# Moving the conversion of w_out to tiles 48 to 70, and two steps of the weight conversion to ScalarE, in a fused attention and gated-convolution kernel

## The chip, the cores and the metric

The kernel runs on one core of a Trainium2 chip. The metric is device time in microseconds (us) of one execution, as the median over several runs. One execution was also profiled; PE is TensorE, DVE is VectorE, ACT is ScalarE, POOL is GpSimd, SP is the engine whose queue issues nearly all DMAs.

## What is computed

```
q_bits = (q @ proj) > 0;  k_bits = (k @ proj) > 0        # 6 bits: a bucket per row
mask   = bucket(q_bits) == bucket(k_bits)
attn   = softmax(where(mask, q @ k.T / sqrt(64), -1e9))  # per batch and head: 768 x 768
x      = attn @ v, heads side by side                    # (4, 768, 512)
gate   = sigmoid(causal depthwise conv of x, 5 taps, conv_w)
out    = ((x @ w_val) * gate) @ w_out
```

There are 4 batches of 8 heads with 768 rows of 64 numbers. `w_val` and `w_out` are 512 x 512 and come as 64-bit floats, as does `conv_w`; everything else is 32-bit.

## The kernel before

**Tiles.** A unit is one (batch, head); there are 32. Each has 6 tiles of 128 query rows, so the main loop runs over 192 tiles k. For each tile PE makes the scores (L266) into a PSUM buffer `s` (two of them), DVE takes the row maxima (L272) and two small numbers from them, `gs` (L278) and `nb` (L282), ACT does the exponential (L290), POOL divides by the row sums (L305), PE transposes the result (L314), ACT copies it out of PSUM (L323), and PE multiplies it with v (L337). The scores of tile k + 1 need the buffer of tile k - 1, so PE can be held by the exponential, that by `nb`, and that by whatever stands ahead of the maxima in DVE's queue. Each engine executes its queue in the order of the program.

**Side work.** The loop advances several generators by a step now and then: `preps` (next unit's operands: L170, L173 on POOL and DMAs on SP's queue), `convs` (the convolution, L366 on POOL and L368 on DVE, and the rounding of x, L357 and L358), `moes` (the two products with the weights, L399 and L424, the first one of a batch from tile 67 on), `ahead` (bits of later units) and `weights`.

**The weight conversion.** Two generators of `load_weights` each take half of the eight parts (four 128-row parts of `w_val`, then four of `w_out`). A part is 128x512 numbers of 64 bits. It goes through seven steps: a DMA on SP's queue (L137); ACT takes the absolute value of the high words (L91, tile `o`); DVE clamps and shifts it (L93, L94); DVE puts the bits of the high words together (L97, in place in `w`); DVE takes the exponent (L100) and multiplies the low words with it and with a constant (L101); DVE casts to the rounded matmul type (L109, out to `wv` or `wo`); POOL makes the remainder (L111, L113). A staging tile `w` has two buffers, so the DMA of a part waits until POOL has finished an earlier one. How many steps a tile takes is a table in the main loop, seven steps per six tiles, turn by turn from the two generators. `outp`, the first user of `wo`, finishes what is left.

Of the kernel before, what the change touches and what calls it, by code (L numbers as in the profile page):

```python
# [10 lines left out]
AF = mybir.ActivationFunctionType  # L11
ALU = mybir.AluOpType
# [4 lines left out]
U32 = mybir.dt.uint32  # L17
# [9 lines left out]
def kernel(  # L27
# [10 lines left out]
    nc = tc.nc  # L38
    B, H, _, S = qk.shape
# [4 lines left out]
    NP = H // 2  # L44
    KW = 5
    LAG = 3
    scale = 1.0 / float(D) ** 0.5
# [15 lines left out]
    op = ctx.enter_context(tc.tile_pool(name="op", bufs=2))  # L63
# [23 lines left out]
    def from_float64(w, t):  # L87

        lo, hi = w[:, :, 0], w[:, :, 1]
        a, d, ti = hi.bitcast(FP32), lo.bitcast(FP32), t.bitcast(I32)  # L90
        nc.scalar.activation(out=t, in_=a, func=AF.Abs)  # L91
        yield
        nc.vector.tensor_scalar(out=t, in0=t, scalar1=LEAST, scalar2=None, op0=ALU.max)  # L93
        nc.vector.tensor_scalar(out=ti, in0=ti, scalar1=3, scalar2=0x3fffffff,  # L94
                                op0=ALU.logical_shift_left, op1=ALU.bitwise_and)
        yield
        nc.vector.scalar_tensor_tensor(out=hi, in0=hi, scalar=-2 ** 30, in1=ti,  # L97
                                       op0=ALU.bitwise_and, op1=ALU.bitwise_or)
        yield
        nc.vector.tensor_scalar(out=ti, in0=hi, scalar1=-2 ** 23, scalar2=None, op0=ALU.bitwise_and)  # L100
        nc.vector.scalar_tensor_tensor(out=d, in0=lo.bitcast(U32), scalar=2.0 ** -52, in1=t,  # L101
                                       op0=ALU.mult, op1=ALU.mult)
        return a, d

    def split_weight(w, hi, lo):
        if w.dtype == I32:
            a, d = yield from from_float64(w, op.tile([P, 512], FP32, name="o"))
            yield
            nc.vector.tensor_copy(out=hi, in_=a)  # L109
            yield  # L110
            nc.gpsimd.tensor_tensor(out=a, in0=a, in1=hi.bitcast(FP32), op=ALU.subtract)  # L111
            yield
            nc.gpsimd.tensor_tensor(out=lo, in0=a, in1=d, op=ALU.add)  # L113
        else:
            nc.scalar.copy(out=hi, in_=w)
            yield
            nc.gpsimd.tensor_tensor(out=lo, in0=w, in1=hi.bitcast(FP32), op=ALU.subtract)
# [10 lines left out]
        else:  # L128
            nc.sync.dma_start(out=cw_sb, in_=conv_w)

    def load_weights(which):
        parts = [(src[:, c, :], hl[0][:, c, :], hl[1][:, c, :])
                 for src, hl in ((w_val, wv), (w_out, wo)) for c in range(NP)]
        for src, hi, lo in parts[which::2]:
            if src.dtype == mybir.dt.int64:
                w = wst.tile([P, 512, 2], I32, name="w64")
                nc.sync.dma_start(out=w, in_=src.bitcast(I32).rearrange("p (n t) -> p n t", t=2))  # L137
            else:
                w = wst.tile([P, 512], FP32, name="w32")
                nc.sync.dma_start(out=w, in_=src)  # L140
            yield
            yield from split_weight(w, hi, lo)

    def load_raw(i):
        if i < len(units):
# [230 lines left out]
    def acc_tile():  # L376
        pools = accs
        pool, name = pools[0]
        pools.append(pools.pop(0))
        if name == "s":  # L380
            return pool.tile([P, 2, 512], FP32, name="s")[:, 0, :]
        return pool.tile([P, 512], FP32, name=name)

    def moe(b, xs_, g):
# [5 lines left out]
                todo.pop(0)()  # L390

        def val(o, j):
            acc = acc_tile()
            m = 0
            for wi, xi in ((0, 0), (1, 0), (0, 1)):
                if m:
                    yield
                for c in range(NP):
                    nc.tensor.matmul(out=acc[:, 0:HS], lhsT=wv[wi][:, c, j * P:(j + 1) * P],  # L399
                                     rhs=xs_[(c, o)][xi], start=(m == 0), stop=(m == 11))  # L400
                    m += 1
                later()
            ht = hp.tile([P, HS], FP32, name="ht", bufs=2)
            nc.vector.tensor_tensor(out=ht, in0=acc[:, 0:HS], in1=g[j][:, o:o + HS], op=ALU.mult)  # L404

            def split():
                hh = hp.tile([P, HS], FP32R, name="hh")
                nc.vector.tensor_copy(out=hh, in_=ht)  # L408
                hl = hp.tile([P, HS], FP32R, name="hl")
                nc.gpsimd.tensor_tensor(out=hl, in0=ht, in1=hh.bitcast(FP32), op=ALU.subtract)  # L410
                hs[(o, j)] = (hh, hl)
            todo.append(split)
            yield
# [48 lines left out]
    def step(gens):  # L462

        while gens:
            try:
                return next(gens[0])
            except StopIteration:
                gens.pop(0)
# [7 lines left out]
    with tc.manual_schedule(engines=ENGINES):  # L476
# [1 line left out]
            load_raw(i)  # L478
        load_values(0)
        first_prep()  # L480
        weights = [[load_conv(), load_weights(0)], [load_weights(1)]]
        preps = [first_bits(), prep(1)]
        scores(0)
        next(preps[1])
# [5 lines left out]
        for k in range(N + LAG + 1):  # L490
# [21 lines left out]
                exponentials(k)  # L512
            if k >= 60 or k % 2:
                step(convs)
            for _ in range((1, 0, 2, 0, 2, 2)[k % 6]):
                step(weights[turn])
                turn = 1 - turn

# [79 lines left out]
```

## Time and profile before

| | |
|---|---|
| median of 3 runs | 622.08 us (621.6 to 622.21) |
| the profiled execution: its span, first to last instruction | 620.8 us |
| PE busy | 585.5 us, 94% of the span |
| DVE busy | 437.6 us, 70% |
| ACT busy | 421.4 us, 68% |
| POOL busy | 395.6 us, 64% |

The profile gives no time of the profiled execution other than its span. A busy share is a mean over stretches that differ: up to tile 66 there is attention alone, with the conversion of the weights beside it, and from tile 67 on the products with the weights fill PE. So the table says little of a change in one stretch.

### The profile page before, as it was taken

The numbers are of one execution on the slowest core, as the hardware profiler recorded it, in microseconds if no ns is written. First come the engines' busy times: TensorE is split into PE (matmuls) and PEld (weight loads), VectorE is DVE, ScalarE is ACT, GpSimd is POOL, SyncE is SP. The second block draws the span as 40 slices with busy tenths as digits, with TensorE's granted clock in tenths as the row PEclk, the third lists the DMA queues.
The fourth block names the chain that finished last, engine by engine and source line by source line (L and its number), as shares of the span: only waits on it lengthen the run. The fifth ranks groups of instructions, "written<-read, shape, count | busy, mean of one in ns | idle before, by whom it ended". The sixth has DMA issues, their size and how long they took to land.

```text
span 620.8 us, 10648 instructions
## 1 busy us (share of the span) xinstructions
PE 585.5 (94%) x3496; PEld 423.4 (68%) x3496; DVE 437.6 (70%) x1017; ACT 421.4 (68%) x881; POOL 395.6 (64%) x373
## 2 busy tenths in 40 slices
PE   5789898989999999999999999999999999999997
PEld 2655565555657777776767777777667877775895
DVE  5869798998975866668575867569665877665532
ACT  2777777778778666777787676777787766765400
POOL 3576868778766765578564777568764777544321
PEclk9799999999999999999999999999999999999999
DMA  6467666564532235243433234333422213200111
GB/s 227 123 197 199 200 167 208 157 175 118 133 83 68 70 79 142 72 108 82 122 82 107 61 80 126 84 115 82 108 70 78 67 42 91 69 18 1 51 52 51
DMA packets 29031, 64.64 MB, mean 104 GB/s; under 512 B 4937, under 2 KB 10057, under 8 KB 28977
## 3 DMA queue, kind: packets, MB, share of 16 engines
q1 hardware_dynamic: 28832, 63.93, 37.8%
q8 instruction: 28, 0.46, 0.3%
q14 instruction: 27, 0.21, 0.1%
q10 hardware_dynamic: 144, 0.03, 0.0%
HBM read 30.60 MB, written 7.86 MB: 62 GB/s over the span
## 4 chain that ended last, share of the span: by engine, by line
PE 66%; DVE 12%; ACT 12%; DMA 5%; issue 3%; POOL 2%; SPq 1%; ACTq 0%; POOLq 0%; DVEq 0%
PE av L337 17%; PE s L266 16%; PE tp L314 12%; PE m L424 8%; PE m L399 7%; ACT p L290 5%; DVE nm L272 4%; ACT pt L323 3%; ACT x L345 2%; DMA w<-in_w_val_dram 2%; DVE g L368 2%; PE tp L399 1%; PE tp L424 1%; PE s L424 1%; DMA bk<-bq 1%
## 5 line engine op out<-in xcount | busy, mean ns | idle before, releaser
L305 POOL TENSOR_SCALAR p<-p,ri 128x768 f32<-128x768 f32 x192 | 210.5, 1100 | 156.0 <-DVE nb L282 130.8
L272 DVE TENSOR_REDUCE nm<-s 128x1 f32<-128x768 f32 x192 | 182.5, 950 | 61.2 <-PE s L266 61.0
L290 ACT ACTIVATE p<-s,nb,gs 128x768 f32<-128x768 f32 x192 | 192.6, 1003 | 46.2 <-DVE nb L282 41.9
L323 ACT COPY pt<-tp 128x384 f32<-128x384 f32 x384 | 165.7, 485 | 75.3 <-PE tp L314 74.4
L314 PEld LDWEIGHTS tp<-ident,p 128*128 128x128 f32 x1152 | 130.3, 142 | 72.2 <-issue 43.6
L314 PE MATMUL tp<-ident,p 128*128 128x128 f32 x1152 | 164.4, 279 | 2.6 <-ACT pt L323 2.1
L337 PE MATMUL av<-pt,vt 128*64 128x384 f32 x768 | 144.9, 498 | 0.0
L266 PE MATMUL s<-ak,aq 76*128 76x384 f32 x384 | 118.1, 389 | 23.2 <-ACT p L290 19.7
L266 PE MATMUL s<-bk,bq 128*128 128x384 f32 x384 | 101.3, 345 | 0.4 <-DVE bq L252 0.4
L337 PEld LDWEIGHTS av<-pt,vt 128*64 128x64 f32 x768 | 47.0, 136 | 61.5 <-issue 61.4
L266 PEld LDWEIGHTS s<-ak,aq 76*128 76x128 f32 x384 | 59.2, 194 | 38.7 <-ACT p L290 34.6
L368 DVE SCALAR_TENSOR_TENSOR g<-x,cw_sb,g 128x768 f32<-128x768 f32 x64 | 79.4, 1241 | 2.2 <-POOL g L366 2.1
L266 PEld LDWEIGHTS s<-bk,bq 128*128 128x128 f32 x384 | 71.7, 194 | 0.8 <-issue 0.8
L173 POOL TENSOR_TENSOR bq<-r,aq 128x768 fp32r<-128x768 f32 x31 | 59.2, 1909 | 0.1
L410 POOL TENSOR_TENSOR hl<-ht,hh 128x384 fp32r<-128x384 f32 x32 | 32.3, 1009 | 39.5 <-DVE hh L408 39.5
L345 ACT COPY x<-av 64x384 f32<-64x384 f32 x64 | 30.4, 475 | 29.7 <-PE av L337 29.0
L282 DVE TENSOR_SCALAR nb<-nm,gs 128x1 f32<-128x1 f32 x192 | 40.4, 211 | 3.5
L399 PE MATMUL m<-xh,wv 128*128 128x384 f32 x200 | 42.7, 337 | 0.0
L358 POOL TENSOR_TENSOR xl<-x,xh 128x384 fp32r<-128x384 f32 x32 | 33.4, 1059 | 13.8 <-DVE xh L357 13.8
L290 ACT ACTIVATION_READ_ACCUMULATOR p<-s,nb,gs 128x1 f32 x192 | 39.0, 203 | 0.0
L404 DVE TENSOR_TENSOR ht<-m,g 128x384 f32<-128x384 f32 x25 | 13.9, 556 | 35.6 <-PE m L399 29.2
L424 PE MATMUL m<-wo,hh 128*128 128x512 f32 x144 | 38.1, 394 | 0.0
(86 smaller groups left out, 486.9 us busy)
## 6 DMA issues: line engine op xcount, KB each, us to landing
r<-in_qk_dram SPq DMA_DIRECT2D x32, 384.0 KB
vt<-in_v_dram SPq DMA_DIRECT2D x16, 384.0 KB
out_dram<-o SPq DMA_DIRECT2D x24, 256.0 KB
ak<-aq SPq DMA_DIRECT2D x31, 192.0 KB
bk<-aq SPq DMA_DIRECT2D x31, 192.0 KB
bk<-bq SPq DMA_DIRECT2D x31, 192.0 KB
bq<-aq SPq DMA_DIRECT2D x31, 192.0 KB
hh<-in_qk_dram SPq DMA_DIRECT2D x16, 192.0 KB
```

Of the source, the lines that this page charges most:

```text
L173: nc.gpsimd.tensor_tensor(out=bq, in0=r, in1=aq.bitcast(FP32), op=ALU.subtract)
L266: nc.tensor.matmul(out=s[:, hf, 0:HS], lhsT=lq[0:n, qs], rhs=rk[0:n, hf * HS:(hf + 1) * HS], start=n == M, stop=n == P)
L272: nc.vector.tensor_reduce(out=nm, in_=s[:, :, 0:HS], axis=AX.XY, op=ALU.max, negate=True)
L290: nc.scalar.activation(out=p, in_=s[:, :, 0:HS], func=AF.Exp, bias=nb, scale=gs.pop(k), accum_out=sm[:, k % 2, 0:1])
L305: nc.gpsimd.tensor_scalar(out=p, in0=p, scalar1=rcs.pop(k), scalar2=1.0, op0=ALU.mult, op1=ALU.mult)
L314: nc.tensor.transpose(out=tp[:, n * P:(n + 1) * P], in_=p[:, kb * P:(kb + 1) * P], identity=ident)
L323: nc.scalar.copy(out=pt[:, :, qo:qo + P], in_=tp[:, 0:HS].rearrange("p (a b) -> p a b", b=P))
L337: nc.tensor.matmul(out=av[s * D:(s + 1) * D, 0:HS], lhsT=vt[:, kb, hh * D:(hh + 1) * D], rhs=pt[kb // 3][:, kb % 3, :], start=(kb == 0), s ...
L345: nc.scalar.copy(out=x[hh * D:(hh + 1) * D, o:o + HS], in_=av[s * D:(s + 1) * D, 0:HS])
L368: nc.vector.scalar_tensor_tensor(out=g, in0=x[:, k:k + S], scalar=w, in1=g, op0=ALU.mult, op1=ALU.add)
L399: nc.tensor.matmul(out=acc[:, 0:HS], lhsT=wv[wi][:, c, j * P:(j + 1) * P], rhs=xs_[(c, o)][xi], start=(m == 0), stop=(m == 11))
L424: nc.tensor.matmul(out=acc, lhsT=hs[(o, j)][hi][:, tb * P:(tb + 1) * P], rhs=wo[wi][:, j, :], start=(m == 0), stop=(m == 11))
```

## The change

Three things are changed. The product on DVE of low words, exponent and constant (L101) becomes two instructions: ACT multiplies the low words by the constant, right behind the absolute value (new L92), and DVE multiplies that with the exponent (new L102, two inputs and no scalar). For `w_val` the cast to the rounded type is done by ACT and not by DVE. And each of the two generators becomes two, one for `w_val` and one for `w_out` behind it, with fewer steps per tile from tile 12 on, so that `w_val` ends at about tile 44 and `w_out` is converted at tiles 48 to 70; `val` finishes the `w_val` part first if it must.

```diff
         nc.scalar.activation(out=t, in_=a, func=AF.Abs)
+        nc.scalar.activation(out=d, in_=lo.bitcast(U32), func=AF.Copy, scale=2.0 ** -52)
         yield
...
-        nc.vector.scalar_tensor_tensor(out=d, in0=lo.bitcast(U32), scalar=2.0 ** -52, in1=t,
-                                       op0=ALU.mult, op1=ALU.mult)
+        nc.vector.tensor_tensor(out=d, in0=d, in1=t, op=ALU.mult)
         return a, d
...
-            nc.vector.tensor_copy(out=hi, in_=a)
+            cast(out=hi, in_=a)
...
         def val(o, j):
+            for gens in weights:
+                while len(gens) > 1:
+                    step(gens)
...
-        weights = [[load_conv(), load_weights(0)], [load_weights(1)]]
+        weights = [[load_weights(i, w_val, wv, nc.scalar.copy), load_weights(i, w_out, wo, nc.vector.tensor_copy)]
+                   for i in range(2)]
+        weights[0].insert(0, load_conv())
...
-            for _ in range((1, 0, 2, 0, 2, 2)[k % 6]):
+            for _ in range((1, 0, 2, 0, 2, 2)[k % 6] if k < 12 else (1, 0, 1, 0, 1, 1)[k % 6] if k < 48 else 1):
                 step(weights[turn])
                 turn = 1 - turn
```

What this does to the queues is seen in the order of the instructions. Line numbers behind L90 differ by one or so between the two kernels.

DVE at tiles 28 and 29, before: maxima are `nm`, the convolution is `g`, and the rows with `w` and `o` are the conversion.

```order
L93 TENSOR_SCALAR o<-o 128x512
L94 TENSOR_SCALAR o<-o 128x512
L109 CAST wv_120<-w_875 128x512
L229 TENSOR_SCALAR ht<-m,packed 128x384
L272 TENSOR_REDUCE nm<-s 128x1
L278 TENSOR_SCALAR gs<-nm 128x1
L282 TENSOR_SCALAR nb<-nm,gs 128x1
L368 SCALAR_TENSOR_TENSOR g<-x,cw_sb,g 128x768
L97 SCALAR_TENSOR_TENSOR w_994<-w_994,o 128x512
```

DVE at tiles 28 and 29, of the change.

```order
L228 TENSOR_SCALAR ht<-m,packed 128x384
L271 TENSOR_REDUCE nm<-s 128x1
L277 TENSOR_SCALAR gs<-nm 128x1
L281 TENSOR_SCALAR nb<-nm,gs 128x1
L367 SCALAR_TENSOR_TENSOR g<-x,cw_sb,g 128x768
```

Four instructions of the conversion no longer stand between these maxima and the next ones.

DVE at tiles 54 and 55, before.

```order
L272 TENSOR_REDUCE nm<-s 128x1
L296 TENSOR_SCALAR s_2166<-sm 128x2
L278 TENSOR_SCALAR gs<-nm 128x1
L300 RECIPROCAL ri<-s_2166 128x2
L282 TENSOR_SCALAR nb<-nm,gs 128x1
L272 TENSOR_REDUCE nm<-s 128x1
L278 TENSOR_SCALAR gs<-nm 128x1
L282 TENSOR_SCALAR nb<-nm,gs 128x1
L368 SCALAR_TENSOR_TENSOR g<-x,cw_sb,g 128x768
```

DVE at tiles 54 and 55, of the change.

```order
L281 TENSOR_SCALAR nb<-nm,gs 128x1
L101 TENSOR_SCALAR o<-w_1865 128x512
L102 TENSOR_TENSOR w_1865<-w_1865,o 128x512
L271 TENSOR_REDUCE nm<-s 128x1
L277 TENSOR_SCALAR gs<-nm 128x1
L281 TENSOR_SCALAR nb<-nm,gs 128x1
L367 SCALAR_TENSOR_TENSOR g<-x,cw_sb,g 128x768
L94 TENSOR_SCALAR o<-o 128x512
L95 TENSOR_SCALAR o<-o 128x512
```

Four instructions of `w_out` now stand here, two of them right behind a convolution step.

ACT at tiles 10 and 11, of the change; before, the row with L92 was not there and the other rows stood in the same order.

```order
L289 ACTIVATE p,sm<-s,nb,gs 128x768
L91 ACTIVATE o<-w_427 128x512
L92 ACTIVATE w_427<-w_427 128x512
L322 COPY pt<-tp 128x3x128 x2
L289 ACTIVATE p,sm<-s,nb,gs 128x768
```

The new multiplication stands ahead of the copies that free PE's transposes, and there are eight such places.

On DVE, before, L93 of a part stands at tiles 4, 11, 16, 23, 28, 35, 40 and 47 and its last L109 at tile 52; in the change the same step (L94 there) stands at tiles 4, 11, 17, 30, 38, 50, 55 and 64 and the last L109 at tile 70. ACT's L91 stands at tiles 2, 10, 14, 22, 26, 34, 38 and 46 before, and at 2, 10, 14, 28, 35, 48, 53 and 62 in the change; its four casts at 8, 18, 26 and 40. PE's order is the same in both, and its first use of `wo` stands behind the scores of tile 78. On SP's queue the load that the L91 of tile 10 reads stood behind the last of the four copies for the next unit (`bq<-aq`); in the change it stands ahead of the third (`bk<-bq`).

## Rows read from the trace of the kernel before

**Rows 1.** The page: span, busy time, and the chain that ended last, by engine.

```profile
span 620.8 us, 10648 instructions
PE 585.5 (94%) x3496; PEld 423.4 (68%) x3496; DVE 437.6 (70%) x1017; ACT 421.4 (68%) x881; POOL 395.6 (64%) x373
...
PE 66%; DVE 12%; ACT 12%; DMA 5%; issue 3%; POOL 2%; SPq 1%; ACTq 0%; POOLq 0%; DVEq 0%
```

**Rows 2.** Busy us by stretch: length, PE, PEld, DVE, ACT, POOL; clock, DMA share, GB/s.

```profile
42.80:76.50 33.70, 31.49 (x206) 19.54 (x205) 27.54 (x67) 25.36 (x55) 24.89 (x23) 1.00 0.67 189
76.50:109.50 33.00, 29.34 (x187) 18.80 (x185) 30.41 (x70) 25.42 (x54) 26.34 (x24) 1.00 0.65 186
109.50:143.90 34.40, 30.83 (x203) 19.14 (x202) 32.81 (x72) 25.30 (x54) 27.59 (x25) 1.00 0.59 167
143.90:175.40 31.50, 28.64 (x182) 18.22 (x181) 26.36 (x60) 24.10 (x52) 24.44 (x25) 1.00 0.45 111
...
159.80:175.40 15.60, 14.05 (x91) 8.97 (x89) 12.28 (x29) 11.90 (x26) 12.89 (x13) 1.00 0.49 130
...
175.40:195.90 20.50, 20.02 (x131) 14.25 (x130) 14.20 (x33) 17.52 (x33) 12.13 (x12) 1.00 0.31 74
195.90:213.20 17.30, 16.39 (x102) 12.23 (x101) 14.15 (x32) 11.89 (x27) 13.17 (x13) 1.00 0.28 73
```

**Rows 3.** ACT's groups in 76.5:109.5 and in 143.9:175.4: the exponentials.

```profile
L290 ACT ACTIVATE p<-s,nb,gs 128x768 f32<-128x768 f32 x12 | 12.0, 1000 | 4.3 <-DVE nb L282 4.3
...
L290 ACT ACTIVATE p<-s,nb,gs 128x768 f32<-128x768 f32 x12 | 12.0, 1000 | 3.4 <-DVE nb L282 3.3
```

**Rows 4.** Stretches again, instructions on tile o alone (DVE, ACT).

```profile
42.80:76.50 33.70, 8.48 (x11) 1.36 (x2) 1.00 0.67 189
76.50:109.50 33.00, 8.08 (x11) 1.35 (x2) 1.00 0.65 186
109.50:143.90 34.40, 9.83 (x11) 1.33 (x2) 1.00 0.59 167
143.90:175.40 31.50, 2.96 (x3) 0.00 (x0) 1.00 0.45 111
```

**Rows 5.** Instructions on tiles w and o: count, duration ns min/median/max.

```profile
L91 ACT ACTIVATE o<-w x8: 662/672/698, 19.1 to 139.6; 128x512 f32<-128x512 f32 x8
L97 DVE SCALAR_TENSOR_TENSOR w<-w,o x8: 680/890/1318, 25.1 to 143.8; 128x512 int32<-128x512 int32 x8
L100 DVE TENSOR_SCALAR o<-w x8: 416/576/827, 27.4 to 147.7; 128x512 int32<-128x512 int32 x8
L101 DVE SCALAR_TENSOR_TENSOR w<-w,o x8: 1273/1276/1281, 27.8 to 148.5; 128x512 f32<-128x512 uint32 x8
L109 DVE CAST wv<-w x4: 409/416/419, 32.1 to 87.2; 128x512 fp32r<-128x512 f32 x4
...
L93 DVE TENSOR_SCALAR o<-o x8: 416/426/1194, 22.3 to 140.3; 128x512 f32<-128x512 f32 x8
L94 DVE TENSOR_SCALAR o<-o x8: 427/1018/1024, 22.7 to 141.5; 128x512 int32<-128x512 int32 x8
```

**Rows 6.** Timeline: start, us, engine, instruction, [idle before and who ended it].

```profile
8.44 0.95 DVE L252 TENSOR_TENSOR bq<-r,aq 64x768 fp32r<-64x768 f32 x1
...
30.82 0.48 SPq L176 DMA_DIRECT2D bk<-bq  x1
...
33.92 0.58 SPq L137 DMA_DIRECT2D w<-in_w_val_dram  x1
...
39.77 0.69 ACT L91 ACTIVATE o<-w 128x512 f32<-128x512 f32 x1 [1.62 <-DMA w<-in_w_val_dram]
...
72.96 0.70 ACT L91 ACTIVATE o<-w 128x512 f32<-128x512 f32 x1 [1.67 <-DMA w<-in_w_val_dram]
...
105.92 0.67 ACT L91 ACTIVATE o<-w 128x512 f32<-128x512 f32 x1 [0.53 <-DMA w<-in_w_out_dram]
```

More of the change, by code (lines that the diff above doesn't have):

```diff
@@ L100, in from_float64, with split_weight @@
         nc.vector.tensor_scalar(out=ti, in0=hi, scalar1=-2 ** 23, scalar2=None, op0=ALU.bitwise_and)
-        nc.vector.scalar_tensor_tensor(out=d, in0=lo.bitcast(U32), scalar=2.0 ** -52, in1=t,
-                                       op0=ALU.mult, op1=ALU.mult)
+        nc.vector.tensor_tensor(out=d, in0=d, in1=t, op=ALU.mult)
         return a, d
-    def split_weight(w, hi, lo):
+    def split_weight(w, hi, lo, cast):
         if w.dtype == I32:
@@ L129, in load_conv, with load_weights @@
             nc.sync.dma_start(out=cw_sb, in_=conv_w)
-    def load_weights(which):
-        parts = [(src[:, c, :], hl[0][:, c, :], hl[1][:, c, :])
-                 for src, hl in ((w_val, wv), (w_out, wo)) for c in range(NP)]
+    def load_weights(which, w_in, hl, cast):
+        parts = [(w_in[:, c, :], hl[0][:, c, :], hl[1][:, c, :]) for c in range(NP)]
         for src, hi, lo in parts[which::2]:
@@ L141, in load_weights @@
             yield
-            yield from split_weight(w, hi, lo)
+            yield from split_weight(w, hi, lo, cast)
     def load_raw(i):
```

## The prediction

> **What bounds the kernel now.** I read the page first. PE is busy 94% of the span, and the chain that ended last lies on PE for 66%, on DVE and on ACT for 12% each [rows 1]. So the change can give only what PE loses by waiting, and the question is where it waits. The stretches answer that [rows 2]. I cut them at the exponentials of tiles 12, 24, 36, 48, 60, 66 and 72, so that the first four hold 12 tiles each. In the three stretches of tiles 12 to 47 PE is busy 91.66 of 101.1 us, so 9.4 us are idle, and DVE is busy 90.76 us, as much as PE. From tile 60 on PE is idle 0.48 of 20.5 and 0.91 of 17.3 us, and DVE has 6.3 and 3.15 us to spare. The conversion of the weights lies in the first stretches: its instructions on tile `o` alone take DVE 8.48, 8.08 and 9.83 us there, and 2.96 us in the fourth [rows 4].
>
> The price of such DVE time can be read from two stretches with the same work otherwise. Tiles 24 to 35 and tiles 48 to 59 have 12 exponentials each [rows 3], by the program four convolution steps on DVE each, and no step of the products; they take 33.0 and 31.5 us [rows 2]. Beside rows 4 there are two casts and one cast of 0.416 us [rows 5], so the conversion takes DVE 8.91 and 3.38 us. So 5.53 us of DVE time go with 1.5 us of time, **0.27 us per us**. The rest is hidden because DVE runs ahead of PE part of the time. That price holds two ACT steps more and a DMA wait of 0.53 us [rows 6] too, so it is rather high than low for DVE alone.
>
> **The change, part by part.**
>
> *The product.* L101 takes 1.276 us, eight times [rows 5]. In its place DVE has a two-input instruction on 128x512. The trace has no such row. The nearest are L252, 0.95 us for 768 columns, so 512/768 of it, 0.63 us [rows 6], and L97 on the same tile, 0.68 to 1.32 us [rows 5]. I take 0.7; the bounds are 0.63 and 1.28 (nothing gained). That is 0.58 us less per part.
>
> *ACT's instructions.* The multiplication by a constant reads whole numbers, which no row of ACT shows. L91 has the same shape and stride and takes 0.672 us; I take that for it and for the cast, and 1.28, what DVE needs for whole numbers, as the upper bound. That is 12 instructions, 8.1 us more on ACT. An ACT instruction costs nothing when ACT would be idle, and all of itself when it stands ahead of the copy or the exponential that PE waits for. ACT is busy 76.08 of 101.1 us at tiles 12 to 47 and 24.10 of 31.5 at 48 to 59 [rows 2], so idle a quarter; the chain has 12% of its time on ACT [rows 1]. Between none and all I take a quarter, near the low one: **2.0 us lost**, bounds 0 and 8.1.
>
> A rule speaks against this part: the Trainium skill, page ScalarE: Activation LUTs, section Rules for kernel authors, says to multiply on VectorE and not on ScalarE. The row agrees for the cast (0.416 us on DVE, 0.672 on ACT). By that rule the 12 instructions are a loss wherever ACT has no time to spare. It becomes a rival below.
>
> *Tiles 12 to 47.* From the order, DVE has these steps left there: L97 four times at 0.89, L100 and the new product four times at 0.58 + 0.7, L93 and L94 three times at 0.43 + 1.02, one cast of 0.42 [rows 5]. That is 3.56 + 5.12 + 4.35 + 0.42 = 13.45 us. Before it is 26.39 us on tile `o` [rows 4] and six casts, 28.9 us. So 15.4 us less, at 0.27: **4.2 us gained**. Bounds: nothing, and the 9.4 us that PE is idle.
>
> *DMA waits.* ACT waits 1.62, 1.67 and 0.53 us for the DMA of a part [rows 6]. Counted in POOL's divisions, the L91 of tiles 22, 34 and 46 stand four behind the POOL step that frees their buffer; the last one waits for nothing, and the DMAs are busy 0.67, 0.65 and 0.59 of these stretches [rows 2]. In the change the L91 of tiles 28 and 35 stand six and five behind, and those of tiles 48, 53 and 62 four behind, where the DMAs are busy 0.45 and 0.31; so I expect no wait. The 0.53 is in the price already. Of the 1.67 I count 0.6, since PE had work in its queue for part of it. At tile 10 the load moves ahead of the `bk<-bq` issued at 30.82, 3.1 us before its old place, more than the wait of 1.62; I count 0.6 again. Its 512 KB now go ahead of two copies of the next unit; those are needed at tile 12, and I take that for hidden by the 8 us between. With the DVE time saved below tile 12 (one product and one cast, 1.0 us, 0.3 at the price): **1.5 us gained**; bounds 0 and 3.6.
>
> *Tiles 48 to 71.* At tiles 48 to 59 the same count gives 1.45 twice, 0.89 twice, 1.28 twice and a cast: 7.66 us, 4.3 more than now, at 0.27: 1.2 us. At tiles 60 to 70 it is 1.45 + 0.89 + 1.28 + 0.83 = 4.45 us where there was nothing. DVE's 6.3 and 3.15 us of idle time cover it; if that cover is gone the price is that above, 1.2 us. I take 0.8, since the idle time comes in pieces. **2.0 us lost**, bounds 0 and 8.8 (all of it). What is queued behind these instructions are the maxima of the next tile, for them the exponential waits, and for that PE's scores.
>
> *What costs nothing.* Four of the eight POOL pairs (L111, L113) move along. POOL is busy 12.89 of 15.6 us at tiles 54 to 59 [rows 2], and the division that is behind them is needed a tile later. The last of `wo` is ready at about tile 74, its first use is at tile 78.
>
> *Sum.* 4.2 + 1.5 - 2.0 - 2.0 = **1.7 us gained**. The profiled span is 620.8 us, 1.28 us under the median of 622.08; I leave that difference as it is: 622.08 - 1.7 = **620.4 us**, 0.27% faster. A measurement of this kernel tells about 0.2% (1.24 us) from no change, so the forecast lies just beyond that.
>
> **The rivals.**
>
> *The idle time has another cause (no change).* For it: in the stretch from 159.8, where DVE has no step of the conversion, PE is idle 1.55 of 15.6 us, 10%, and at tiles 12 to 47 it is 9.4 of 101.1, 9% [rows 2]. Then what holds PE is the loop from scores over maxima and exponential back to the buffer, at any load. Against it: the same work takes 1.5 us longer at tiles 24 to 35. With a price of 0.1, tiles 12 to 47 give 1.5, the DMA waits 1.3, tiles 48 to 71 cost 0.9, ACT 2.0: 622.2 us.
>
> *DVE was the bound (much faster).* For it: DVE is as busy as PE at tiles 36 to 47, 32.81 of 34.4 us. If most of PE's idle time goes, tiles 12 to 47 give 7 us, and with the rest as in the forecast it is 622.08 - 7 - 1.5 + 4.0 = 617.6 us. Against it: DVE is idle 6.16 us in the first of these three stretches, and PE 2.2 there.
>
> *The new place is not covered (slower).* Tiles 54 to 57 get 1.28 + 1.45 + 0.42 + 0.89 = 4.0 us between maxima and maxima, two of them right behind a convolution step; DVE is busy 12.28 of 15.6 us there already [rows 2], so it would be over 100% with them. If the 8.8 us of tiles 48 to 71 are paid at 0.7 and not 0.23, they cost 6.1 us: 624.5. It decides (slower by over 0.2%) from 4.9 us on, a price of 0.56. Against it: tiles 28 to 31 have those four kinds of steps now, and their stretch pays 0.27.
>
> *ACT is in the way (slower).* Each of the 12 instructions stands ahead of the copies that free PE's transposes. If all are paid in full, 8.1 and not 2.0 us: 626.5. This is where the rule of the page ScalarE: Activation LUTs would lead. Against it is a quarter of ACT idle.
>
> **How the numbers follow.** Forecast (619 to 620.8) 0.30; much faster 0.19; no change, with what falls between 620.8 and 623.3, 0.31; new place not covered 0.15; ACT 0.05. So faster 0.49, same 0.31, slower 0.20. The time is that of the forecast. The range goes from a little under the much faster case, 617.0, to 623.6, which leaves out most of the two slower cases and the far end of the fast one, together 0.2. The forecast's own range is 619 to 621.8, by the bounds of ACT's share and of the price.
>
> **What would show it.** Right: tiles 12 to 47 take some 97 us and not 101.1 (4.2 and 0.6 less, and half of ACT's 2.0 more), with no ACT wait for a weight DMA there; tiles 48 to 71 take about 72 us and not 69.3; the new product takes 0.63 to 0.8 us on DVE, L92 about 0.67 on ACT. Wrong: PE's idle share at tiles 12 to 47 stays at 9%, or the stretch of tiles 54 to 59 grows by over 3 us, or PE's scores wait longer for exponentials that wait for L92 or a cast.

## The result, and the profile after

The changed kernel takes 629.96 us (median of 4 runs, 628.25 to 630.82), the kernel before in the same runs 622.14 (621.6 to 623.71): a ratio of 1.0115, 95% interval 1.0094 to 1.0135. It is slower by 1.15%, and outside of the range that was given.

The page of the changed kernel, the lines that answer to [rows 1]:

```profile
span 626.5 us, 10663 instructions
PE 588.0 (94%) x3496; PEld 424.3 (68%) x3496; DVE 442.4 (71%) x1013; ACT 427.4 (68%) x894; POOL 395.8 (63%) x373
...
PE 68%; DVE 12%; ACT 12%; DMA 3%; issue 2%; POOL 1%; SPq 0%; ACTq 0%; POOLq 0%; DVEq 0%
```

DVE was to have less work, and has 442.4 us, not 437.6. The stretches of the changed kernel, from a view as in [rows 2], cut at the exponentials of tiles 12, 24, 36, 48, 54, 60, 66, 72 and 78; the first begins at 12 us:

```profile
12.00:43.60 31.60, 27.08 (x134) 19.66 (x127) 23.66 (x64) 22.92 (x49) 15.81 (x16) 0.78 0.55 152
...
43.60:75.40 31.80, 30.96 (x206) 19.47 (x205) 25.04 (x63) 25.67 (x56) 20.95 (x20) 1.00 0.69 191
75.40:107.10 31.70, 29.23 (x184) 18.45 (x183) 26.01 (x61) 26.67 (x58) 24.73 (x25) 1.00 0.68 187
107.10:140.70 33.60, 30.51 (x200) 18.84 (x200) 29.34 (x65) 24.40 (x54) 22.81 (x22) 1.00 0.52 146
140.70:158.00 17.30, 15.33 (x96) 9.47 (x95) 13.52 (x32) 14.20 (x32) 11.92 (x13) 1.00 0.55 147
158.00:175.60 17.60, 14.74 (x94) 9.46 (x94) 17.27 (x36) 12.16 (x27) 13.38 (x12) 1.00 0.29 86
175.60:200.10 24.50, 20.61 (x130) 14.12 (x128) 20.17 (x38) 18.66 (x34) 17.25 (x15) 1.00 0.35 90
200.10:217.40 17.30, 16.03 (x98) 12.12 (x99) 16.19 (x34) 11.92 (x27) 13.88 (x13) 1.00 0.28 73
217.40:237.00 19.60, 17.95 (x110) 13.47 (x109) 14.61 (x31) 12.26 (x28) 16.82 (x15) 1.00 0.36 86
```

Tiles 12 to 47 take 97.1 us and not 101.1: 4.0 gained, as forecast. Tiles 48 to 71 take 76.7 and not 69.3: 7.4 lost, where the forecast was about 72 us. Tiles 72 to 77 hold no DVE step of the conversion, and lose 1.6 more. The first stretch is 0.8 us longer; its clock is 0.78, before 0.89, since the granted clock falls to its lower level (1.2 of 2.4 GHz) twice there and not once. From tile 78 on both kernels run alike. 0.8 - 4.0 + 7.4 + 1.6 = 5.8, and the spans differ by 5.7. The medians differ by 7.8: the profiled execution of the changed kernel took 628.25 us, the least of its four, and what the others lose beyond it is in no trace of this kernel (see the clock, below).

The stretches again, instructions on tile `o` alone, as in [rows 4]:

```profile
43.60:75.40 31.80, 5.82 (x8) 0.67 (x1) 1.00 0.69 191
75.40:107.10 31.70, 3.88 (x5) 1.36 (x2) 1.00 0.68 187
107.10:140.70 33.60, 4.73 (x6) 0.00 (x0) 1.00 0.52 146
140.70:158.00 17.30, 2.89 (x5) 1.33 (x2) 1.00 0.55 147
158.00:175.60 17.60, 6.33 (x6) 0.00 (x0) 1.00 0.29 86
175.60:200.10 24.50, 2.04 (x3) 0.67 (x1) 1.00 0.35 90
200.10:217.40 17.30, 2.62 (x2) 0.00 (x0) 1.00 0.28 73
```

The same kinds of instructions on `w` and `o` as in [rows 5] (count, ns min/median/max):

```profile
L92 ACT ACTIVATE w<-w x8: 661/674/700, 18.8 to 184.1; 128x512 f32<-128x512 uint32 x8
L98 DVE SCALAR_TENSOR_TENSOR w<-w,o x8: 681/686/1491, 24.2 to 197.7; 128x512 int32<-128x512 int32 x8
L101 DVE TENSOR_SCALAR o<-w x8: 416/666/1274, 26.5 to 205.8; 128x512 int32<-128x512 int32 x8
L102 DVE TENSOR_TENSOR w<-w,o x8: 1275/1280/1377, 26.9 to 207.1; 128x512 f32<-128x512 f32 x8
...
L109 DVE CAST wo<-w x4: 418/441/2080, 137.1 to 211.4; 128x512 fp32r<-128x512 f32 x4
```

The new product (L102) takes 1.28 us, as long as the old one. ACT's multiplication takes 0.67, as forecast. And one instruction takes anything from its least time to three or five times that: L101 0.42 to 1.27, the cast 0.42 to 2.08. Two places of the timeline show what stands beside the long ones and what follows (tiles 60 to 63, and 72 to 75):

```profile
178.31 2.54 POOL L172 TENSOR_TENSOR bq<-r,aq 128x768 fp32r<-128x768 f32 x1
179.09 2.08 DVE L109 CAST wo<-w 128x512 fp32r<-128x512 f32 x1
181.05 0.98 DVE L271 TENSOR_REDUCE nm<-s 128x1 f32<-128x768 f32 x1
182.57 0.99 ACT L289 ACTIVATE p<-s,nb,gs 128x768 f32<-128x768 f32 x1 [1.49 <-DVE nb L281]
183.70 0.62 PE L265 MATMUL s<-ak,aq 76*128 76x384 f32 x2 [0.82 <-ACT p L289]
...
219.02 1.30 POOL L111 TENSOR_TENSOR w<-w,wo 128x512 f32<-128x512 f32 x1
220.28 2.59 POOL L172 TENSOR_TENSOR bq<-r,aq 128x768 fp32r<-128x768 f32 x1
221.10 1.98 DVE L410 CAST hh<-ht 128x384 fp32r<-128x384 f32 x1
225.30 0.99 ACT L289 ACTIVATE p<-s,nb,gs 128x768 f32<-128x768 f32 x1 [1.53 <-DVE nb L281]
226.44 0.62 PE L265 MATMUL s<-ak,aq 76*128 76x384 f32 x2 [1.65 <-ACT p L289]
```

The kernel before, at tiles 72 to 73, where POOL has no L111 (the `bq` instruction is L173 there, the cast L408):

```profile
214.10 1.83 POOL L173 TENSOR_TENSOR bq<-r,aq 128x768 fp32r<-128x768 f32 x1
217.55 0.35 DVE L408 CAST hh<-ht 128x384 fp32r<-128x384 f32 x1
```

The moved pair of POOL instructions pushes L172 back until it stands beside DVE's cast of `hh`, which then takes 1.98 and not 0.35 us; the maxima behind it are late, the exponential waits 1.53 and PE 1.65. So tiles 72 to 77 lose time through POOL, with none of the conversion on DVE.

### The profile page after: what moved, and what is told of

Same layout as the page of the kernel before. It is cut to its first block, busy times and chain, and to the rows that moved or that the text cites. A ratio compares the mean times of both kernels' runs of the same rounds, so it can differ in the third digit from the quotient of the medians.

```text
span 626.5 us, 10663 instructions
## 1 busy us (share of the span) xinstructions
PE 588.0 (94%) x3496; PEld 424.3 (68%) x3496; DVE 442.4 (71%) x1013; ACT 427.4 (68%) x894; POOL 395.8 (63%) x373
## 4 chain that ended last, share of the span: by engine, by line
PE 68%; DVE 12%; ACT 12%; DMA 3%; issue 2%; POOL 1%; SPq 0%; ACTq 0%; POOLq 0%; DVEq 0%
PE av L336 18%; PE s L265 17%; PE tp L313 13%; PE m L426 8%; PE m L401 6%; ACT p L289 5%; DVE nm L271 4%; ACT pt L322 3%; ACT x L344 2%; DVE g L367 2%; PE tp L401 1%; PE tp L426 1%; PE s L426 1%; PE s L401 1%; DVE nb L281 1%
## 5 line engine op out<-in xcount | busy, mean ns | idle before, releaser
L172 POOL TENSOR_TENSOR bq<-r,aq 128x768 fp32r<-128x768 f32 x31 | 61.1, 1972 | 0.1
L406 DVE TENSOR_TENSOR ht<-m,g 128x384 f32<-128x384 f32 x25 | 13.9, 555 | 31.9 <-PE m L401 26.9
```

What stands on the lines that cost most here:

```text
L172: nc.gpsimd.tensor_tensor(out=bq, in0=r, in1=aq.bitcast(FP32), op=ALU.subtract)
```

## The experiments

Lengths of the stretches in the profiled executions, in us, each from exponential to exponential. A star marks those in which the granted clock was at its lower level for a part. Each row is one execution, and not always near the median: that of e3 took 628.33 us, where the median of ten is 624.41.

| tiles | 12-47 | 48-53 | 54-59 | 60-65 | 66-71 | 72-77 |
|---|---|---|---|---|---|---|
| before | 101.1 | 15.9 | 15.6 | 20.6 | 17.3 | 17.9 |
| changed | 97.1 | 17.2 | 17.7 | 24.5 | 17.3 | 19.5 |
| e1 | 101.9 | 15.9 | 15.6 | 20.6 | 17.3 | 17.9 |
| e2 | 96.6 | 16.0 | 18.3 | 24.5 | 17.3 | 19.5 |
| e3 | 95.9 | 20.7* | 18.1* | 22.2 | 17.3 | 19.1 |
| e4 | 96.7 | 16.0 | 18.3 | 24.5 | 18.9* | 21.1* |
| e5 | 97.2 | 17.2 | 17.4 | 22.8 | 18.6* | 18.4 |
| e6 | 97.1 | 16.9 | 17.3 | 23.7 | 18.9* | 19.3 |
| e7 | 95.9 | 18.9 | 18.1* | 21.3 | 17.3 | 18.0 |
| e8 | 106.6* | 16.2 | 16.4 | 21.5 | 17.3 | 17.9 |
| e9 | 97.1 | 16.5 | 20.7* | 24.5 | 18.9* | 21.1* |
| e12 | 107.5* | 15.9 | 15.6 | 22.1 | 17.3 | 17.9 |
| e13 | 105.5* | 15.9 | 15.6 | 21.7 | 17.3 | 17.9 |
| e14 | 104.6* | 16.2 | 18.0* | 21.4 | 17.3 | 17.9 |
| e15 | 105.8* | 19.4* | 16.6 | 22.0 | 17.3 | 17.9 |
| e16 | 97.6 | 18.0 | 19.3* | 22.0 | 17.3 | 17.9 |

**Which part of the change.** e1 has the new instructions in the old places (one generator each for both weights, the old table):

```diff
-            for _ in range((1, 0, 2, 0, 2, 2)[k % 6] if k < 12 else (1, 0, 1, 0, 1, 1)[k % 6] if k < 48 else 1):
+            for _ in range((1, 0, 2, 0, 2, 2)[k % 6]):
```

> The new instructions alone (ACT's multiplication in all eight parts and ACT's cast for w_val), with the steps of the conversion where the kernel before has them. If the place of w_out is what costs (theory), this stays near the kernel before: 622 to 624 us, since DVE loses only four casts and ACT gets 8 us in places a quarter of which are on the path. If ACT's new instructions are what costs (rival), it is at 627 us or more.

Measured: 623.05 us, ratio 1.0003 (0.9989 to 1.0018). ACT's twelve instructions, the new product and the four casts that DVE gives up come, taken together, to nothing that can be measured.

e2 has the old instructions in the new places (and all casts on DVE again):

```diff
-        nc.scalar.activation(out=d, in_=lo.bitcast(U32), func=AF.Copy, scale=2.0 ** -52)
...
-        nc.vector.tensor_tensor(out=d, in0=d, in1=t, op=ALU.mult)
+        nc.vector.scalar_tensor_tensor(out=d, in0=lo.bitcast(U32), scalar=2.0 ** -52, in1=t,
+                                       op0=ALU.mult, op1=ALU.mult)
```

> The new places alone, with the product and all casts on DVE as in the kernel before. If the place of w_out costs (theory): 627 to 630 us, with tiles 12 to 47 at 97 to 99 us and tiles 48 to 77 some 8 us longer than before. If ACT's new instructions cost (rival): 621 us or less.

Measured: 628.07 us, ratio 1.0081 (1.0057 to 1.0104). The place alone makes the loss, in nearly the same stretches as the whole change. Its ten executions spread: the four with a mean granted clock of 0.993 or more took 625.3 to 626.3 us, the six at 0.983 to 0.991 627.8 to 630.3.

e4 is the changed kernel with the old product, and without L92, for `w_out` alone:

```diff
+        if old:
+            nc.vector.scalar_tensor_tensor(out=d, in0=lo.bitcast(U32), scalar=2.0 ** -52, in1=t,
+                                           op0=ALU.mult, op1=ALU.mult)
+        else:
             nc.vector.tensor_tensor(out=d, in0=d, in1=t, op=ALU.mult)
```

> The changed kernel, in which the w_out parts take the old product on DVE, so that the four ACT multiplications of tiles 35 to 62 are gone. DVE's product took 1.276 us before and its new one takes 1.280 us, so DVE's time stays. Theory (DVE): 628.5 to 630 us, at most 1 us less than the changed kernel. Rival (ACT): 4 us less or more, some 626 us.

Measured: 629.28 us, ratio 1.0087 (1.0053 to 1.0121). ACT's L92 in the new place is not the cause.

**What costs in the new place.** e3 is the changed kernel with DVE's four steps of `w_out` on 8 columns, so that most of the conversion of `w_out` is left out:

```diff
+        lo, hi, t = lo[:, 0:n], hi[:, 0:n], t[:, 0:n]
...
+            a, d = yield from from_float64(w, op.tile([P, 512], FP32, name="o"), n=8 if cast == nc.vector.tensor_copy else None)
```

> The changed kernel, in which the four arithmetic steps on DVE (clamp and shift, bits, exponent, product) of the w_out parts work on 8 of 512 columns; order, waits, DMAs, ACT and POOL work stay, and the numbers of w_out come out otherwise. If it is DVE's time at tiles 48 to 70 that costs (theory): some 7 us less than the changed kernel, 621 to 624 us. If it is the ACT or the POOL instructions or the DMAs there: 628 to 630 us as now.

e5 does the same with POOL's two:

```diff
+            if cast == nc.vector.tensor_copy:
+                a, d, hi, lo = (x[:, 0:8] for x in (a, d, hi, lo))
             nc.gpsimd.tensor_tensor(out=a, in0=a, in1=hi.bitcast(FP32), op=ALU.subtract)
...
+        nc.gpsimd.memset(wo[1].bitcast(FP32), 0.0)
         first_prep()
```

> The changed kernel, with the two POOL instructions of each part of w_out (L111 and L113) on 8 of 512 columns; the low part of w_out is set to zero once at the start, where POOL is idle 4 us, and so most of it is left out of the result. Theory one (the four POOL pairs, 2.3 us each, push POOL's long two-input instructions L172 onto DVE's casts, which then take 2 us instead of 0.4, and delay the division): tiles 72 to 77, which hold no DVE step of the conversion, come back from 19.5 to about 18 us, tiles 60 to 65 from 24.5 to about 22.5, and the kernel takes about 626.5. Rival (only DVE's own steps cost; POOL has room): tiles 72 to 77 stay at 19.5 and the kernel at 629 to 630.

e7 has both edits.

> The changed kernel, with DVE's four arithmetic steps and POOL's two steps of each part of w_out on 8 of 512 columns (the low part is set to zero at the start); only the loads, ACT's two instructions and DVE's cast of w_out stay whole. Theory one (DVE and POOL together make the cost of the new place): tiles 48 to 77 take some 88.5 us, within 1.5 us of the 87.2 of the kernel before and not 96.2, the 4 us gained at tiles 12 to 47 stay, and the kernel takes about 620.5 (619.5 to 622). Rival (ACT's instructions and the loads of w_out cost there too): tiles 48 to 77 stay above 90.5 us and the kernel takes 623 or more, as with DVE's steps alone cut short (624.4).

Measured: e3 624.41 us, ratio 1.0019 (1.0 to 1.0039); e5 624.27, 1.0025 (1.0007 to 1.0043); e7 620.97, 0.9968 (0.9952 to 0.9983). The stretches of tiles 60 to 65 and 72 to 77 in e3, in e5 and in e7:

```profile
178.60:200.80 22.20, 20.36 (x132) 14.29 (x130) 17.44 (x38) 18.67 (x36) 14.98 (x14) 1.00 0.33 85
...
218.10:237.10 19.00, 17.79 (x110) 13.44 (x109) 13.51 (x31) 12.14 (x27) 16.23 (x15) 1.00 0.37 88
```

```profile
173.40:196.10 22.70, 20.74 (x132) 14.29 (x129) 18.47 (x38) 18.59 (x35) 14.44 (x15) 1.00 0.34 89
...
214.70:233.00 18.30, 17.79 (x110) 13.44 (x109) 13.24 (x31) 12.15 (x27) 14.71 (x15) 1.00 0.39 92
```

```profile
174.20:195.50 21.30, 20.38 (x132) 14.36 (x130) 16.11 (x38) 18.54 (x36) 10.82 (x13) 1.00 0.31 84
...
212.80:230.80 18.00, 17.86 (x110) 13.52 (x109) 12.46 (x31) 12.21 (x28) 14.42 (x15) 1.00 0.39 93
```

At tiles 60 to 65 cutting DVE's part gives back 2.3 of the 24.5 us, cutting POOL's 1.7, both 3.2; what is left is 0.7 over the kernel before. At tiles 72 to 77 POOL's part alone gives 1.1 of the 1.6, DVE's 0.4. In e3 the cast of `hh` takes 0.35 us again, but now POOL's `bq` instruction (1.81 us from 220.40) stands beside a convolution step, which takes 1.01 us at its shortest, and the stretch still loses 1.2 us:

```profile
220.81 2.21 DVE L369 SCALAR_TENSOR_TENSOR g<-x,cw_sb,g 128x768 f32<-128x768 f32 x1
```

So in these two stretches the two engines make the cost together, and POOL's part of it was not in the prediction.

For tiles 48 to 59, where the change loses 3.4 us, this is not shown: they stay long in e3, in e5 and in e7. Cutting to 8 columns does not take DVE's time away: the product still takes 0.81 to 0.99 us beside POOL in e3, and all of tile `o` 7.3 us at tiles 48 to 71, of 13.9. In e7 tiles 48 to 77 took 93.6 us and not the 88.5 expected, though its total, and the gain at tiles 12 to 47, held. There ACT waited 2.35 us for the load of a part that its earlier end had brought nearer, and the clock was low for a part. The changed kernel has a wait at the same place, tile 48, of 0.66 us, and PE waits 0.87 us there for ACT's copies; how the rest of the 3.4 us is shared stays open.

e6 is the changed kernel with the casts of `w_out` on ACT too:

```diff
-load_weights(i, w_out, wo, nc.vector.tensor_copy)
+load_weights(i, w_out, wo, nc.scalar.copy)
```

> The changed kernel, with the rounded parts of w_out cast by ACT too, as those of w_val are; nothing is left out. Theory one (the cast of w_out on DVE took 2.08 us once, beside POOL's L172, and delayed the maxima behind it): tiles 54 to 59 come back from 17.7 to about 16.3 us, and the kernel takes about 628.5. Rival (ACT has no time to spare there, and what DVE gives up ACT loses): tiles 54 to 59 stay at 17.7 or more, and the kernel takes 630 to 631.

Measured: 625.12 us, ratio 1.0046 (1.0022 to 1.007). Faster than the change, by more than either theory said, but not where theory one said: tiles 54 to 59 took 17.3, tiles 60 to 65 gave 0.8. In the profiled executions 2.4 us more lie ahead of tile 12 (its exponential starts at 41.29 and not at 43.65 us), where e6's clock was low for less long. How much of the median's 4.8 us is the cast and how much the clock stays open.

**Where the steps stand.** e9 takes the steps of tiles 48 to 59 in even tiles:

```diff
-                           if k < 48 else 1):
+                           if k < 48 else (2, 0)[k % 2] if k < 60 else 1):
```

> The changed kernel, with the steps of tiles 48 to 59 taken two at a time in the even tiles, and none in the odd ones, which hold a convolution step each; nothing is left out. The DVE steps of tiles 55, 57 and 59 go to tiles 54, 56 and 58, so that the gap between the maxima of tiles 54 and 55 holds L101, L102, L94 and L95, 2.9 us. Theory one (a conversion step costs where it stands with a convolution step between two maxima): tiles 54 to 59 come back from 17.7 to 16.6 us or less, and the kernel takes 628.5 or less. Rival (what counts is the DVE time in one gap, whatever it is made of): 2.9 us in one gap are as long as a tile, tiles 54 to 59 take 17.7 or more, and the kernel 630 or more.

Measured: 630.89 us, ratio 1.0117 (1.0076 to 1.0158), tiles 54 to 59 20.7 us. DVE's timeline between the maxima of tiles 54 and 55:

```profile
154.92 0.42 DVE L101 TENSOR_SCALAR o<-w 128x512 int32<-128x512 int32 x1
155.38 1.28 DVE L102 TENSOR_TENSOR w<-w,o 128x512 f32<-128x512 f32 x1
156.57 2.05 DVE L94 TENSOR_SCALAR o<-o 128x512 f32<-128x512 f32 x1
158.65 1.02 DVE L95 TENSOR_SCALAR o<-o 128x512 int32<-128x512 int32 x1
```

The four took 4.8 us and not 2.9. Without a convolution step among them, the exponential of tile 55 waits 4.42 us for DVE and PE 3.04 us for that exponential. So theory one fails, and the rival holds: what counts is DVE's time in one gap. How much of the 20.7 us is that alone is not shown, since the clock falls there too, for 6.8 us.

e8 takes one step in every tile from tile 12 on, with all casts on ACT:

```diff
-            for _ in range((1, 0, 2, 0, 2, 2)[k % 6] if k < 12 else (1, 0, 1, 0, 1, 1)[k % 6] if k < 48 else 1):
+            for _ in range((1, 0, 2, 0, 2, 2)[k % 6] if k < 12 else 1):
```

> The instructions of the change with all casts on ACT, but one step of the conversion in every tile from tile 12 on, so that it ends with a POOL step at tile 60 and has DVE steps only up to tile 56; nothing is left out. Theory one (what costs is work beside the products and the convolution from tile 54 on, and an even rate up to there costs little): 1.5 to 2 us gained at tiles 12 to 47, 1 us lost at tiles 48 to 59, nothing from tile 60 on; 621.5 us, not to be told from the kernel before. Rival (each us of DVE time behind tile 48 is paid at 0.7): the 4 us of DVE steps at tiles 52 to 56 cost 2.8; 623.5 us.

Measured: 630.36 us, ratio 1.0125 (1.0101 to 1.0149). Both theories missed. The loss is not behind tile 48: tiles 12 to 47 took 106.6 us, tiles 24 to 35 alone 38.4. ACT waited 3.23 us for a load at 86.58, and the clock fell twice in that stretch. e14 is the same with a third staging buffer for `w`, and four buffers for the raw rows to make room; e12 (four raw buffers) is its control, and e13 (four raw, three staging) takes only the load waits from the kernel before:

```diff
-    raw = ctx.enter_context(tc.tile_pool(name="raw", bufs=5))
+    raw = ctx.enter_context(tc.tile_pool(name="raw", bufs=4))
...
-    wst = ctx.enter_context(tc.tile_pool(name="wst", bufs=2))
+    wst = ctx.enter_context(tc.tile_pool(name="wst", bufs=3))
```

> The kernel before, with four buffers and not five for the raw rows of q and k, as the control of the next run, which needs that space. Expected by both theories: no change, 622 to 623, with the waits of ACT for the weight DMAs at tiles 10, 22 and 34 as before (1.6, 1.7 and 0.5 us); the units' rows are then loaded later, and if that is too late, tiles 0 to 11 get longer.

> The kernel before, with four buffers for the raw rows and three staging buffers for the weights, so that the load of a part need not wait until POOL has finished the part two ahead of it; the work and its places are as before. Theory one (the waits of ACT for those loads, 1.67 and 0.53 us at tiles 12 to 35, hold PE for about as long, and made some 2 of the 4 us that the change gained at tiles 12 to 47, so that 15 us less on DVE were worth only about 2, 0.12 us each): tiles 12 to 23 take 31.8 to 32.3 us and not 33.8, tiles 36 to 47 stay at 34.3, and the kernel takes 1.5 to 3.5 us less than its control. Rival (the 4 us came from DVE's time at 0.27 each, and PE had work in its queue for most of the waits): tiles 12 to 23 stay above 33 us, and the kernel is within 0.8 us of its control.

> The kernel with one conversion step in every tile from tile 12 on (which took 630.4 us, with a wait of ACT of 3.2 us for a load at tile 28), with four buffers for the raw rows and three staging buffers. Theory one (its loss came from the loads, not from the rate): no wait of ACT for a load over 0.3 us, tiles 24 to 35 take 32 to 33 us and not 38.4, and the kernel takes 621 to 624. Rival (one step in every tile is bad in itself, since it puts two DVE instructions behind a convolution step in odd tiles): tiles 24 to 35 stay above 35 us, and the kernel takes 627 or more.

Measured: e12 628.56 us (626.65 to 629.4), e13 627.54 (627.08 to 628.54), e14 629.04 (628.76 to 633.03). The control was not neutral: the fifth raw buffer is worth 6 us, and the three are compared with each other alone. Without any load wait (e13) tiles 12 to 35 took 66.5 us, in the control 67.4 with 1.2 us of them, and before [rows 2] 66.7 with 2.2. So those waits cost little, and most of the 4 us of the change came from the steps. e14 had no load wait, and tiles 24 to 35 still took 36.6 us against 33.1 in e13. One gap makes most of it, with a convolution step, two casts of x, L101 and L102, together 4.4 us of DVE time between two maxima:

```profile
107.00 0.61 PE L265 MATMUL s<-ak,aq 76*128 76x384 f32 x2 [3.70 <-ACT p L289]
```

The even rate is bad there for its own places, as in e9. It is not shown for tiles 12 to 47 as a whole, which took 104.6 us in e14 and 105.5 in e13, where the clock was low at other tiles.

e15 and e16 take five steps per six tiles at tiles 12 to 47, with the kernel's own instructions, and the old rate behind; they differ in one tile of six:

```diff
-            for _ in range((1, 0, 2, 0, 2, 2)[k % 6]):
+            for _ in range((1, 0, 2, 0, 2, 2)[k % 6] if k < 12 or k >= 48 else (1, 0, 1, 0, 2, 1)[k % 6]):
```

> The kernel before with its own instructions and casts, and five steps of the conversion per six tiles and not seven at tiles 12 to 47; what is left follows at the old rate and ends with DVE's last cast at tile 62; nothing is left out. Theory one (a lighter rate gives back part of the 4 us, and steps cost much only from tile 54 on, where this has 2 parts and not 3 and a half of w_out): 2 us gained at tiles 12 to 47, 1 to 2 us lost at tiles 48 to 63, none at 72 to 77: 621 to 622.5. Rival (any step behind tile 54 costs more than one at tiles 12 to 47 gives): 624 or more.

> The same rate as the run before (five steps per six tiles at tiles 12 to 47, the kernel's own instructions), with the two-step tile put earlier, so that POOL frees the staging buffers two tiles earlier (tiles 36 and 42, not 38 and 44) and the absolute values of tiles 41 and 47 stand five tiles behind that and not three; nothing is left out. There ACT waited 2.20 and 3.26 us for those loads, and TensorE's granted clock fell to half for 6.8 us behind each. Theory one (those two waits and what the clock did behind them were the loss): no wait over 0.7 us, no low-clock stretch at tiles 36 to 53, tiles 36 to 47 take 33 to 34.5 us and not 40.4, and the kernel takes 621 to 624. Rival (the rate itself loses, by steps beside convolution or POOL): tiles 36 to 47 stay above 37 us, and the kernel takes 627 or more.

Measured: e15 633.18 us, ratio 1.0178 (1.0149 to 1.0207); e16, with `(1, 0, 2, 0, 1, 1)`, 626.0 us, 1.0052 (1.0032 to 1.0072). In e15 ACT waits for a load, PE behind it for ACT, and then the clock falls (the timeline, and stretches of 0.5 us, with the clock in the third column from the end):

```profile
125.55 0.66 ACT L91 ACTIVATE o<-w 128x512 f32<-128x512 f32 x1 [2.20 <-DMA w<-in_w_out_dram]
126.72 1.02 PE L314 MATMUL tp<-ident,p 128*128 128x128 f32 x6 [2.21 <-ACT pt L323]
```

```profile
126.50:127.00 0.50, 0.28 (x3) 0.31 (x3) 0.50 (x1) 0.50 (x3) 0.50 (x1) 1.00 0.88 172
130.00:130.50 0.50, 0.50 (x4) 0.23 (x2) 0.50 (x1) 0.00 (x0) 0.50 (x1) 0.50 0.00 0
134.00:134.50 0.50, 0.50 (x4) 0.41 (x3) 0.00 (x0) 0.50 (x2) 0.00 (x0) 0.91 0.82 246
```

The wait at 147.21, 3.26 us, is followed by the same. e16 has neither, and tiles 36 to 47 take 32.8 us and not 40.4: theory one there. Its total is over what that theory said, since tiles 48 to 59 lose 5.8 us (18.0 and 19.3, the clock low for a part). It keeps 3.5 us at tiles 12 to 47 and loses more behind; no rate that was tried beats the kernel before.

**The product.** e10 was run once to see the product alone:

```diff
+        if form == 1:
+            yield
+        out = t if form >= 2 else d
-        nc.vector.tensor_tensor(out=d, in0=d, in1=t, op=ALU.mult)
-        return a, d
+        nc.vector.tensor_tensor(out=out, in0=d, in1=t, op=ALU.mult)
+        return a, out
```

> The changed kernel, with the product on DVE in four forms, to see what its 1.28 us are made of; nothing is left out. First half of w_val: a step later than the exponent, otherwise as it is. Second half of w_val: a step later, and out to the contiguous tile o and not back into the low words, which lie 8 bytes apart. First half of w_out: right behind the exponent, out to o. Second half of w_out: the low words from a contiguous tile too, all three operands contiguous. Theory one (the 8-byte stride in and out makes it 1.28): 1.28 in the first form, 0.6 to 0.9 in the others. Rival (it waits for the instruction just before it, whose output it reads): 0.7 in the two forms of w_val, 1.28 in the two of w_out. Second rival (two 32-bit inputs cost that anyhow, and L97's 0.68 is due to its integer type): 1.28 in all four.

The kernel that ran differs from this text for `w_val`: its first half is as in the change, its second half a step later and still in place. The forms of `w_out` are as told. DVE and POOL beside three of the products (L109 here; L105 is the exponent):

```profile
87.65 0.69 DVE L109 TENSOR_TENSOR w<-w,o 128x512 f32<-128x512 f32 x1
...
140.57 1.08 POOL L311 TENSOR_SCALAR p<-p,ri 128x768 f32<-128x768 f32 x1
140.91 1.28 DVE L109 TENSOR_TENSOR o<-low,o 128x512 f32<-128x512 f32 x1
...
186.38 0.42 DVE L105 TENSOR_SCALAR o<-w 128x512 int32<-128x512 int32 x1
186.83 0.69 DVE L109 TENSOR_TENSOR o<-low,o 128x512 f32<-128x512 f32 x1
```

All three theories fail. The same contiguous form takes 1.28 us beside POOL's division and 0.69 beside an idle POOL, right behind the exponent both times; and in place, with a stride, it takes 0.69 when POOL is idle (87.65). The product is 0.69 us, and the rest is POOL's. The old product is no longer than that either: once in e15 and once in e16 it meets an idle POOL:

```profile
165.85 0.69 DVE L101 SCALAR_TENSOR_TENSOR w<-w,o 128x512 f32<-128x512 uint32 x1
```

e11 gives each DVE instruction a step of its own, never two in a tile, with all casts on ACT and the conversion ending at tile 54; a step tells by "V" that the next one is DVE's:

```diff
         nc.vector.tensor_scalar(out=t, in0=t, scalar1=LEAST, scalar2=None, op0=ALU.max)
+        yield "V"
...
+            for _ in range((2, 1, 2, 1, 2, 2)[k % 6]):
+                if dve and kind[turn]:
+                    turn = 1 - turn
+                if dve and kind[turn]:
+                    break
```

> The instructions of the change with all casts on ACT, in about the old places (the conversion ends at tile 54), and each of DVE's five instructions of a part in a step of its own, never two of them in one tile; nothing is left out. In the runs so far the first conversion instruction of a step starts at once behind the exponential's factors and takes 0.42 (L94, L101) or 0.68 us (L98, L102), and the second one, which meets POOL's division that the same factors release, 1.02 (L95) or 1.28 us (L102). Theory one (the second instruction waits for POOL's, so DVE's time for a part is 2.6 us alone and 4 us in pairs): L95 0.43, L102 0.69 us, DVE busy 10 us or more under the kernel before, and at the price of tiles 24 to 35, 0.27, 2 to 4 us faster than before: 618 to 620. Rival (what DVE saves POOL waits for, since the two still stand side by side, or DVE's time there is no bound): 621.5 to 623, no change.

Measured: 640.74 us, ratio 1.0288 (1.026 to 1.0315). The product now has a median of 0.698 us, as theory one says; L95 0.705, over the 0.43 that it says. But a part stays in its staging buffer longer, and ACT waits 18.1 us for seven loads. So the experiment does not tell what DVE's time is worth.

## Why the prediction was wrong

**The step that failed** is "Tiles 48 to 71 ... 2.0 us lost". Both of its factors were too small. DVE's work: 8.8 us more were counted at the mean durations of [rows 5]. Measured, tile `o` has 2.89 + 6.33 + 2.04 + 2.62 = 13.88 us there and the three casts 0.42 + 2.08 + 0.42 = 2.92, against 3.38 before ([rows 4] and a cast), 13.4 us more. The durations had grown where POOL stood beside them (the product 1.28, one cast 2.08). The price: 7.4 us for it, 0.55 per us, and with tiles 72 to 77 9.0, 0.67; not 0.23. Nor is it one price: tiles 48 to 59 lose 3.4 us for 6.3 more on DVE (0.54), tiles 60 to 65 3.9 for 4.1 (nearly all), tiles 66 to 71 nothing for 3.0. That tiles 48 to 59 pay twice the 0.27 that was read from tiles 24 to 35, with as many convolution steps and no products, is measured and not explained. The sentence "DVE's 6.3 and 3.15 us of idle time cover it" does not hold for tiles 60 to 65, which pay most; it does for 66 to 71, which take 17.3 us in both kernels.

**The rival "the new place is not covered"** had the cause on DVE's side: a price of 0.7 at tiles 48 to 71, though it named tiles 54 to 57, and tiles 60 to 65 pay most. POOL's side was in no rival. At the DVE time as measured that is 13.4 * 0.7 = 9.4 us. It was given a chance of 0.15.

**"What costs nothing"** failed for POOL. It was weighed by busy time, and the division behind the pairs was not late; but POOL's L172 moved until it stood beside DVE's casts. Of the cuts of one engine, e5 gives back the most at tiles 72 to 77.

**The product** was put at 0.7 us and is 0.69 by itself (e10), but 1.28 where it stands, since POOL's division is released by the same small numbers. The 1.276 of the old product, eight times within 8 ns [rows 5], was such a wait too (0.69 in e15 and e16), and not what DVE needs for whole numbers, as the bound for ACT had it; L97, 0.68 to 1.32 on the same tile, showed both cases. The Trainium skill, page SBUF — State Buffer, section Who interferes with whom, states this: a DVE instruction with two SBUF inputs, or a cast or tensor_scalar in its fast mode, shares a port pair with GpSimd, and whoever comes first holds it while the other blocks. The traces agree (0.69 and 1.28 us, 0.42 and 2.08). By that rule the bound "nothing gained" was the value to take.

**Tiles 12 to 47** came out as said: 97.1 us. DVE has 14.43 us on tile `o` and one cast where it had 26.39 and six, 14.0 us less (15.4 forecast), so 4.0 us are 0.29 per us against 0.27. e2 shows that the place alone gives it, e13 that the load waits give little of it. The fit is in part luck: the product gave none of the 2.3 us of DVE time counted for it there, other instructions took less than their medians in [rows 5], and ACT's share of the loss did not come.

**ACT's instructions** were put at 2.0 us lost and cost nothing measurable (e1). L92 takes 0.67 us, as taken. The Trainium skill, page ScalarE: Activation LUTs, section Rules for kernel authors, says to multiply on VectorE. It decided nothing here: ACT's multiplication takes 0.67 us and DVE's product alone 0.69, and the casts, 0.67 us on ACT and 0.42 on DVE, cost nothing in e1.

**DMA waits**: 1.5 us gained. The waits at tiles 10 to 47 did go, and one of 0.66 us came at tile 48, where none was expected. But e13 and its control differ by 1.0 us with ranges that overlap, so no run shows that the waits gave 1.5 us.

**The clock** was in no term. In the profiled execution it costs about 0.8 us before tile 12; in others more, as the spread of e2 shows. In e15 it falls behind a wait of PE that a load causes. The same is seen in the new place: in e4 and in e9 PE waits 1.7 us at tile 66 and 1.6 at tile 74, as long as in the changed kernel (1.74 and 1.65 us), and the clock falls within 1.5 us behind each wait; those stretches take 18.9 and 21.1 us and not 17.3 and 19.5. Such falls could account for the 2.1 us between the difference of the medians and that of the spans; no trace of the changed kernel shows it. Why the same waits are not followed by a fall in the profiled executions of the changed kernel and of e2 stays open, and so does what brings it in the first 12 tiles.

## What to carry to other kernels

A price of "us lost per us of an engine's work", read in one stretch, holds for that stretch: the same work cost 0.29 per us at tiles 12 to 47, 0.54 at tiles 48 to 59, nearly all of itself at tiles 60 to 65 and nothing at tiles 66 to 71, and DVE's durations themselves grew on the way. What counts is DVE's time between one maximum and the next, gap by gap, and not its busy share. Before moving DVE work, look at what POOL runs beside it at the old and at the new place, and take an instruction whose duration has two values in the profile as one that waits. A single value is no proof of the contrary: the old product showed 1.276 us eight times. A lighter rate of a staged side job moves its buffer's release too, so count how far each load stands from the step that frees its buffer.

## What was not expected of the hardware

DVE's cast of 128x512 took 0.42 us and, beside POOL's two-input instruction of 128x768, 2.08; the cast of 128x384 0.35 and 1.98; the product 0.69 and 1.28. POOL's instruction grew too, from 1.83 to 2.59 us. And where PE had waited 2.2 us for ACT, the granted clock was at 0.50 within some 3 us after PE went on, and back near full some 7 us after, though PE was busy nearly all of that time.
